# Weight preparation of a two-stage attention and gated-MLP kernel: earlier first loads, steps placed inside the stages, and another block order

## The chip, the cores and the metric

The kernel runs on one core of one Trainium2 chip. The metric is the device time of one execution in microseconds (us); less is better. The engines are named as the profile names them: PE is TensorE (matmuls; PEld its weight loads), DVE is VectorE, ACT is ScalarE, POOL is GpSimd, and SP is the engine from which every DMA of this kernel is issued. Each engine takes its instructions strictly in the order in which the kernel emits them.

## The reference

Two things are computed one after the other, all in 32-bit floating point, for 8 batch entries, 12 heads, 448 positions and head width 64:

```python
scores = scale * np.matmul(q, k.transpose(0, 1, 3, 2)) - np.log(S)
attn = 1.0 / (1.0 + np.exp(-scores))
x = np.matmul(attn, v)                       # heads side by side: 8 x 448 x 768

h = np.maximum(x @ w_in, 0.0)                # w_in: 768 x 1024
u, v = (h[..., :512], h[..., 512:])
v_n = (v - mu) / np.sqrt(var + 1e-06)        # mean and variance over the 512
v_s = np.einsum('ts,bsd->btd', w_spatial, v_n) + b_spatial[None, :, None]
out = (u * v_s) @ w_out                      # w_out: 512 x 768
```

## The kernel before, in words

**Precision.** Most products are made of three matmuls: each operand is split into a rounded high part and the low remainder (`split`, L98), and high times high, low times high and high times low are summed. So every weight has to be prepared on the chip before it can be used: it arrives as a raw 1024-word block in a work buffer, is converted by bit operations (`convert`, L107 to L133), and is written as a high and a low half into a constant tile. w_in and w_out arrive as 64-bit floating point, w_spatial as 32-bit.

**The stages.** The outer loop runs over four pairs of batch entries, m = 0 to 3. For each pair:

- *attention*: six iterations, each for two pairs of heads. In an iteration, scores for 7 key tiles are made on PE (psc; L226 for the short tile, L244 for the others), ACT takes the sigmoid (L252), and PE multiplies with v (pav, L282). The q/k blocks of the next iteration are cast and split (L100 and L101, tile qks), and the result is split into the constant tile x_s (L288 on ACT, L261 on DVE). The first two q/k blocks are used unsplit.
- *gate values* (`gate_values`): x times the second half of w_in, for seven tiles of 128 rows in four groups, (0,1), (2,3), (4,5) and (6). PE makes pv, ACT the relu rv (L315), DVE the statistics (L319, L320) and the subtraction of the mean (L325), POOL the reciprocal root (L322, L323), and DVE the normalised vn (L335, L336).
- *spatial* (`spatial`), for each of the two batch entries, in two pairs of output chunks: w_spatial times vn in PSUM (pg), then g = pg + bias on DVE (L372).
- *gated* (`gated`): x times the first half of w_in (pu), then g = relu(pu) * g on DVE (L394), then split into gs.
- *output* (`output`): gs times w_out (po) in three pairs of output chunks, copied by ACT (L422) and stored.

**Weights.** `weight_steps` is a Python generator over 22 steps: the six blocks of the gate half of w_in with four of w_spatial between them, six blocks of the other half of w_in, and six of w_out. It loads two steps ahead (`AHEAD`), through three work buffers (tag tmp for the first 13 steps, tag raw, shared with the q/k blocks, for the rest). Each `next` emits a part of a step up to the next `yield`. The first 13 steps (three parts for a block of w_in, one for a block of w_spatial, 31 in all) run on DVE alone: L113, L124, L127, then L129, L132, then L179, L180. The other nine have four parts: L113 and L120 on DVE; L122 on ACT; L129 and L132 on DVE; L176 on ACT. Their last subtraction (L180, DVE) is emitted together with the first part of the step behind.

In m = 0, `attention` asks for the 31 parts: two after the first scores, and then three at two places of every iteration, up to a budget. The main loop asks for four parts (`YB`) after each of the four gate groups, each spatial pair and each gated pair.

**What holds the order.** `in_program_order` binds every engine to the order of emission. PSUM is given out by rotation: three double buffers (ps2) for psc, pv, pg, pu and po, and two single ones (ps1) for pav. So the first pu of a pair takes the buffer of the fourth gate group, free when that group's rv has been read; the second pu takes that of the first spatial pair, free when its g has been added. DMAs all leave one queue, SP, in order; a DMA that waits for its work buffer holds those behind it.

**Block order of the weights.** A block of the first half of w_in holds all 512 output columns for 128 rows of the input; a pu product over all 768 rows for one chunk of 128 output columns therefore reads all six blocks. A block of w_out holds 512 consecutive values of the row-by-row flattened (4 x 768) columns.

Of the kernel before, what the change touches and what calls it, by code (L numbers as in the profile page):

```python
# [35 lines left out]
def attn_gmlp_kernel(  # L36
# [103 lines left out]
    def weight_steps():  # L140

        steps = []
        for i in range(NCC):
            steps += [(w_in, w_in_s, NCC + i)] + [(w_sp, w_sp_s, i)] * (i < NFC)
        steps += [(w_in, w_in_s, i) for i in range(NCC)]
        steps += [(w_out, w_out_s, i) for i in range(NFC * DM // 512)]
        raws = {}

        def load(n):
            if n < len(steps):  # L150
                src, _, i = steps[n]
                w = 512 if src is w_sp else 1024

                if n < NFIRST:
                    raw = work.tile([P, 1024], U32, tag="tmp", name=f"wraw_{n}", bufs=3)[:, :w]
                else:
                    raw = work.tile([P, 1024], U32, tag="raw", name=f"wraw_{n}", bufs=3)
                raws[n] = raw.bitcast(F32) if src is w_sp else raw
                nc.sync.dma_start(raws[n], src[:, i * w : (i + 1) * w])

        for n in range(AHEAD):
            load(n)
        for n, (src, dst, i) in enumerate(steps):
            load(n + AHEAD)
            if src is w_sp and i == 0:
                nc.sync.dma_start(b_bc, b_sp.broadcast_to([P, 512]))
            hi, lo = dst[:, i, 0], dst[:, i, 1]
            scalar = n >= NFIRST
            val = raws.pop(n)
            if src is not w_sp:  # L170
                raw = val
                val = work.tile([P, 512], U32, tag="wval", name=f"wval_{n}", bufs=2)
                yield from convert(val, raw, scalar)
                val = val.bitcast(F32)
            if scalar:
                nc.scalar.copy(hi, val)  # L176
                yield
            else:
                nc.vector.tensor_copy(hi, val)  # L179
            nc.vector.tensor_sub(lo, val, hi.bitcast(F32))  # L180
            if not scalar:
                yield
# [7 lines left out]
    def load_weights(n):  # L190
        for _ in range(n):
            next(weights, None)
# [98 lines left out]
    def product(ps, pairs, more=(), start=True, stop=True):  # L291

        ops = [(st(a), mv(c)) for st, mv in pairs for a, c in TERMS] + list(more)
        for i, (st, mv) in enumerate(ops):
            nc.tensor.matmul(ps, st, mv, start=start and i == 0, stop=stop and i == len(ops) - 1)  # L295

    vns = {}

    def gate_values(m, ts):

        n = len(ts)
        pv = banks(f"pv_{m}_{ts[0]}")
        for i, t in enumerate(ts):
            product(
                pv[:, i, :F],
                [
                    (
                        lambda a, cc=cc, t=t: x_s[:, a, cc, t * P : (t + 1) * P],
                        lambda c, cc=cc: w_in_s[:, NCC + cc, c, :],
                    )  # L310
                    for cc in range(NCC)
                ],
            )
        rv = work.tile([P, 2, 512], F32, tag="tmp", name=f"rv_{m}_{ts[0]}", bufs=3)
        nc.scalar.activation(rv[:, :n], pv[:, :n], AF.Relu)  # L315
        mv = work.tile([P, 2, 2], F32, tag="mv", name=f"mv_{m}_{ts[0]}")
        for i in range(n):
            stats = work.tile([P, 6], F32, tag="stats", name=f"stats_{m}_{ts[i]}")
            nc.vector.bn_stats(stats, rv[:, i])  # L319
            nc.vector.bn_aggr(mv[:, i], stats)  # L320
        rstd = work.tile([P, 2], F32, tag="rstd", name=f"rstd_{m}_{ts[0]}")
        nc.gpsimd.tensor_scalar_add(rstd[:, :n], mv[:, :n, 1], 1e-6)  # L322
        nc.gpsimd.tensor_tensor(rstd[:, :n], rstd[:, :n], mhalf[:, :n], op=ALU.pow)  # L323
        for i in range(n):
            nc.vector.tensor_scalar_sub(rv[:, i], rv[:, i], mv[:, i, 0:1])  # L325
        for i, t in enumerate(ts):
            vn = work.tile([P, 2, 512], F32R, tag="big", name=f"vn_{m}_{t}", bufs=7)
            if t != NFULL:
                parts = [(vn[:, 0], vn[:, 1], slice(0, P))]
            else:  # L330

                a, c = slice(0, HALF), slice(HALF, P)
                parts = [(vn[a, 0], vn[c, 0], a), (vn[c, 1], vn[a, 1], c)]
            for hi, lo, rows in parts:
                nc.vector.tensor_scalar_mul(hi, rv[rows, i], rstd[rows, i : i + 1])  # L335
                nc.vector.scalar_tensor_tensor(  # L336
                    lo,
                    rv[rows, i],
                    rstd[rows, i : i + 1],
                    hi.bitcast(F32),  # L340
                    op0=ALU.mult,
                    op1=ALU.subtract,
                )
            vns[t] = vn

    def cols_of(b):
        return slice(0, S) if b % 2 else slice(512 - S, 512)
# [3 lines left out]
    def spatial(b, fcs):  # L351

        odd = b % 2
        cols = cols_of(b)
        pg = banks(f"pg_{b}_{fcs[0]}")
        for i, fc in enumerate(fcs):
            fs = slice(fc * P, (fc + 1) * P)
            pairs = []
            for c in range(NFULL):
                vn = vns[c + 4 if odd else c]  # L360
                pairs.append(
                    (lambda a, vn=vn: vn[:, a, fs], lambda p, c=c: w_sp_s[:, c, p, cols])
                )

            short = vns[NFULL][:, odd, fs]
            product(
                pg[:, i, :S], pairs, [(short, w_sp_s[:, NFULL, a, cols]) for a in range(2)]
            )
        g = work.tile([P, 2, 512], F32, tag="tmp", name=f"g_{b}_{fcs[0]}", bufs=3)[:, :, :S]
        bb = b_bc[:, cols]  # L370
        bb = bass.AP(bb.tensor, bb.offset, [list(bb.ap[0]), [0, 2], list(bb.ap[1])])
        nc.vector.tensor_add(g, pg[:, :, :S], bb)  # L372
        gates[b, fcs] = g
# [3 lines left out]
    def gated(b, fcs, copy=nc.scalar.copy):  # L377

        odd = b % 2
        g = gates.pop((b, fcs))  # L380
        pu = banks(f"pu_{b}_{fcs[0]}")
        for i, fc in enumerate(fcs):
            fs = slice(fc * P, (fc + 1) * P)
            product(
                pu[:, i, :S],
                [
                    (
                        lambda a, cc=cc: w_in_s[:, cc, a, fs],
                        lambda c, cc=cc: x_s[:, c, cc, odd * S : (odd + 1) * S],
                    )  # L390
                    for cc in range(NCC)
                ],
            )
        nc.vector.scalar_tensor_tensor(g, pu[:, :, :S], 0.0, g, op0=ALU.max, op1=ALU.mult)  # L394
        gs = work.tile([P, 2, 2 * S], F32R, tag="split", name=f"gs_{b}_{fcs[0]}", bufs=3)
        gs = gs.rearrange("p a (i s) -> p a i s", i=2)
        split(gs[:, 0], gs[:, 1], g, copy)
        for i, fc in enumerate(fcs):
            hidden[b, fc] = gs[:, :, i]

    def output(b, es, parts=1):

# [2 lines left out]
        for part in range(parts):  # L405
            for i, e in enumerate(es):

                def weight(a, fc, e=e):
                    block, col = divmod(fc * DM + e * P, 512)
                    return w_out_s[:, block, a, col : col + P]  # L410

                product(
                    po[:, i, :S],
                    [
                        (lambda a, fc=fc: weight(a, fc), lambda c, fc=fc: hidden[b, fc][:, c])
                        for fc in range(part * n, (part + 1) * n)
                    ],
                    start=part == 0,
                    stop=part == parts - 1,
                )  # L420
# [17 lines left out]
    def attention(m):  # L438
# [20 lines left out]
        for n in range(first, end, 2):  # L459
# [20 lines left out]
            scores(n, odds)  # L480
            if direct:
                loads()
                weigh(2)
            ahead(attention_splits, n + 2, end)
            ahead(attention_splits, n + 3, end)
            vals(n, evens + short)
            weigh(3)
        vals(end - 2, odds)

    start_loads(0)  # L490
    pairs = [(0, 1), (2, 3)]
    running = attention(0)
    for m in range(B // 2):
        for _ in running:
            pass
        for ts in ((0, 1), (2, 3), (4, 5), (6,)):
            gate_values(m, ts)
            load_weights(YB)
        b0, b1 = 2 * m, 2 * m + 1
        more = m < B // 2 - 1  # L500
        for fcs in pairs:
            spatial(b0, fcs)
            load_weights(YB)
        for fcs in pairs:
            gated(b0, fcs)
            load_weights(YB)
        for fcs in pairs:
            spatial(b1, fcs)
            load_weights(YB)
        start_loads(m + 1)  # L510
        output(b0, (0, 1))
        output(b0, (2, 3))
# [64 lines left out]
```

## Time and profile before

| | us |
|---|---|
| runs before (three) | 708.11, 708.66, 708.86; median 708.66 |
| the profiled execution, its own time | 708.37 |
| its span, first to last instruction | 706.6 |
| PE busy | 686.4 |
| DVE busy | 283.1 |
| ACT busy | 250.3 |
| mean granted PE clock | 0.990 of full speed |

How to read the lines. In the chain of waits, a row is start, length, engine, tile, line and number of instructions. In the timeline, a row is start, length, engine, line, operation, output and inputs with their shapes, the number of instructions merged, and in brackets the idle time of the engine before it with what ended it. In a list of waits, the numbers are total time, times and longest. In a table of windows, a row is the window, its length, the busy time and number of instructions of the engine asked for, the granted PE clock as a share of full speed, the share of time in which the DMA engines were busy, and GB/s. PE's matmuls are pipelined, so their starts can lie 0.1 to 0.2 us apart from one view to another.

### The profile page before, as it was taken

To read this page: it belongs to the slowest core of one execution; us is meant where nothing else is said; L and a number is where in the kernel's file an instruction comes from. 1 tells how busy PE (TensorE), PEld (TensorE's weight loads), DVE (VectorE), ACT (ScalarE), POOL (GpSimd) and SP (SyncE) were. 2 spreads that over 40 slices of the span, in tenths; PEclk is the share of its full clock that TensorE was granted. 3 is DMA by queue.
4 is the path that set the end of the run, shared out by engine and by line. 5 is a ranking of instruction groups with operands and counts; after the bars stand their busy time and mean duration, and the time that the engine had idled before them with its cause. 6 is when DMAs were issued, how large, how long until landed. Compare 5 with 4: busy or idle time off the path is not lost.

```text
span 706.6 us, 8992 instructions
## 1 busy us (share of the span) xinstructions
PE 686.4 (97%) x3820; PEld 504.7 (71%) x3820; DVE 283.1 (40%) x448; ACT 250.3 (35%) x298; POOL 18.5 (3%) x36
## 2 busy tenths in 40 slices
PE   6899997989999999999999999999999999999997
PEld 2445686979855458899885447899986445889996
DVE  0899376761242416531313423633032441462120
ACT  6688211321366731011237771101125774101111
POOL 0000011000000001100000000100000000110000
PEclk9999998999999999999999999999999999999999
DMA  6675001241334210001234230000233230000102
GB/s 247 211 241 203 1 30 60 90 130 53 111 124 157 88 70 1 1 0 53 79 104 157 91 145 1 1 0 1 79 105 130 101 109 1 1 1 0 53 27 78
DMA packets 20248, 55.37 MB, mean 78 GB/s; under 512 B 1904, under 2 KB 8048, under 8 KB 20208
## 3 DMA queue, kind: packets, MB, share of 16 engines
q1 hardware_dynamic: 20208, 54.80, 22.3%
q8 instruction: 30, 0.49, 0.3%
q14 instruction: 10, 0.08, 0.0%
HBM read 43.78 MB, written 11.01 MB: 78 GB/s over the span
## 4 chain that ended last, share of the span: by engine, by line
PE 78%; DVE 3%; ACT 1%; issue 1%; ACTq 0%
PE po L295 16%; PE pav L282 15%; PE pu L295 14%; PE pv L295 12%; PE psc L244 10%; PE pg L295 8%; PE psc L226 2%; DVE wval L129 0%; DVE wval L132 0%; ACT wraw L122 0%; DVE gs L101 0%; DVE g L394 0%; DVE w_out_s L180 0%; DVE g L372 0%; ACT gs L100 0%
## 5 line engine op out<-in xcount | busy, mean ns | idle before, releaser
L252 ACT ACTIVATE at<-psc,bias_s 128x896 f32<-128x896 f32 x168 | 156.6, 1008 | 40.5 <-PE psc L226 25.3
L282 PE MATMUL pav<-at,v 128*64 128x448 f32 (+1 forms) x768 | 141.2, 553 | 0.0
L295 PE MATMUL po<-gs,w_out_s 128*128 128x448 f32 x576 | 122.2, 372 | 3.2 <-ACT w_out_s L176 2.6
L295 PE MATMUL pu<-x_s,w_in_s 128*128 128x448 f32 x576 | 120.4, 370 | 4.2 <-ACT rv L315 4.2
L295 PEld LDWEIGHTS po<-gs,w_out_s 128*128 128x128 f32 x576 | 109.1, 190 | 15.5 <-ACT w_out_s L176 2.9
L295 PEld LDWEIGHTS pu<-x_s,w_in_s 128*128 128x128 f32 x576 | 110.2, 191 | 13.4 <-ACT rv L315 4.5
L295 PE MATMUL pv<-w_in_s,x_s 128*128 128x512 f32 x504 | 115.4, 390 | 0.0
L295 PEld LDWEIGHTS pv<-w_in_s,x_s 128*128 128x128 f32 x504 | 94.3, 188 | 22.3 <-issue 2.8
L244 PEld LDWEIGHTS psc<-qks 64*128 64x128 f32 x828 | 73.1, 186 | 43.7 <-ACT at L252 16.8
L244 PE MATMUL psc<-qks 64*128 64x448 f32 x828 | 98.7, 379 | 4.4 <-DVE qks L101 4.4
L282 PEld LDWEIGHTS pav<-at,v 128*64 128x64 f32 (+1 forms) x768 | 42.2, 135 | 78.8 <-issue 73.9
L261 DVE TENSOR_TENSOR x_s<-pav,x_s 128x448 fp32r<-128x448 f32 x48 | 30.0, 624 | 126.8 <-ACT x_s L288 126.7
L295 PE MATMUL pg<-w_sp_s,vn 128*128 128x448 f32 x352 | 72.8, 365 | 0.0
L295 PEld LDWEIGHTS pg<-w_sp_s,vn 128*128 128x128 f32 x352 | 66.0, 187 | 5.8
L394 DVE SCALAR_TENSOR_TENSOR g<-pu,g 128x896 f32<-128x896 f32 x16 | 17.4, 1091 | 122.9 <-PE pu L295 122.9
L422 ACT COPY osb<-po 128x896 f32<-128x896 f32 x24 | 21.8, 909 | 121.5 <-PE po L295 110.9
L101 DVE TENSOR_TENSOR qks<-raw,qks 128x832 fp32r<-128x832 f32 x46 | 46.7, 1024 | 1.2
L100 ACT CAST gs<-g 128x896 fp32r<-128x896 f32 x12 | 11.3, 943 | 100.2 <-DVE g L394 100.2
L288 ACT CAST x_s<-pav 128x448 fp32r<-128x448 f32 x48 | 25.6, 534 | 55.4 <-PE pav L282 55.0
L315 ACT ACTIVATE rv<-pv 128x1024 f32<-128x1024 f32 (+1 forms) x16 | 14.7, 919 | 83.5 <-PE pv L295 83.5
L319 DVE BATCH_NORM_STATS2 stats<-rv 128x6 f32<-128x512 f32 x28 | 19.0, 679 | 49.3 <-ACT rv L315 49.3
L100 DVE CAST qks<-raw 128x832 fp32r<-128x832 f32 x36 | 21.1, 587 | 35.5 <-PE po L295 35.3
(36 smaller groups left out, 238.6 us busy)
## 6 DMA issues: line engine op xcount, KB each, us to landing
raw<-qk_dram SPq DMA_DIRECT2D x48, 448.0 KB, 3.6
v<-v_dram SPq DMA_DIRECT2D x24, 448.0 KB, 4.1
out_dram<-osb SPq DMA_DIRECT2D x24, 448.0 KB, 2.6
wraw<-w_in_dram SPq DMA_DIRECT2D x12, 512.0 KB, 4.0
wraw<-w_out_dram SPq DMA_DIRECT2D x6, 512.0 KB, 3.6
wraw<-w_sp_dram SPq DMA_DIRECT2D x4, 256.0 KB, 3.8
b_bc<-b_sp_dram SPq DMA_DIRECT2D x1, 256.0 KB, 3.6
```

What stands on the lines that cost most here:

```text
L100: copy(hi, src)
L101: nc.vector.tensor_sub(lo, src, hi.bitcast(F32))
L244: nc.tensor.matmul(psc[:, j, :S], st[rows, k : k + P], mv[rows, FULL:PART], start=i == 0, stop=i == len(ops) - 1,)
L252: nc.scalar.activation(at, psc[:, :, :S], AF.Sigmoid, bias=bias_s, scale=QK)
L261: nc.vector.tensor_sub(*late.pop(0))
L282: nc.tensor.matmul(pav[heads, :S], vt[rows, t, heads], at[rows, j], start=start, stop=stop)
L288: nc.scalar.copy(x[:, 0], pav)
L295: nc.tensor.matmul(ps, st, mv, start=start and i == 0, stop=stop and i == len(ops) - 1)
L315: nc.scalar.activation(rv[:, :n], pv[:, :n], AF.Relu)
L319: nc.vector.bn_stats(stats, rv[:, i])
L394: nc.vector.scalar_tensor_tensor(g, pu[:, :, :S], 0.0, g, op0=ALU.max, op1=ALU.mult)
L422: nc.scalar.copy(osb, po[:, :, :S])
```

## The change

The generator gets a `yield` right behind its first two loads, and the main program calls it once right behind the first q/k and v loads, so these two weight loads stand ahead of the fourth q/k load. In attention, the two parts after the first scores go. The calls of the main loop move into the stages: in a gate group, two parts ahead of the relu, one ahead of the vn operations, and one behind the first vn of the group; in a spatial pair, four parts ahead of g; in a gated pair, two ahead of g, one ahead of the split and one behind it. The number of parts per stage stays.

The host lays the first half of w_in and all of w_out out by pairs of output chunks: three blocks hold all that the first two chunks of u need, the next three what the last two need; and two blocks of w_out each hold all for one pair of output chunks. `half_of` finds chunk o's weights for row block k in the new order.

```diff
@@ weight_steps
         for n in range(AHEAD):
             load(n)
+        yield
         for n, (src, dst, i) in enumerate(steps):
             load(n + AHEAD)
@@
+    def half_of(w, o, k, n):
+
+        block, col = divmod((o // 2 * n + k) * 2 + o % 2, 4)
+        return w[:, block, :, col * P : (col + 1) * P]
+
@@ gate_values
                     for cc in range(NCC)
                 ],
             )
+        load_weights(2)
         rv = work.tile([P, 2, 512], F32, tag="tmp", name=f"rv_{m}_{ts[0]}", bufs=3)
...
             nc.vector.tensor_scalar_sub(rv[:, i], rv[:, i], mv[:, i, 0:1])
+        load_weights(1)
         for i, t in enumerate(ts):
...
             vns[t] = vn
+            if t % 2 == 0:
+                load_weights(1)
@@ spatial
                 pg[:, i, :S], pairs, [(short, w_sp_s[:, NFULL, a, cols]) for a in range(2)]
             )
+        load_weights(YB)
         g = work.tile([P, 2, 512], F32, tag="tmp", name=f"g_{b}_{fcs[0]}", bufs=3)[:, :, :S]
@@ gated
-                        lambda a, cc=cc: w_in_s[:, cc, a, fs],
+                        lambda a, cc=cc: half_of(w_in_s, fc, cc, NCC)[:, a],
...
+        load_weights(2)
         nc.vector.scalar_tensor_tensor(g, pu[:, :, :S], 0.0, g, op0=ALU.max, op1=ALU.mult)
+        load_weights(1)
         gs = work.tile([P, 2, 2 * S], F32R, tag="split", name=f"gs_{b}_{fcs[0]}", bufs=3)
         gs = gs.rearrange("p a (i s) -> p a i s", i=2)
         split(gs[:, 0], gs[:, 1], g, copy)
         for i, fc in enumerate(fcs):
             hidden[b, fc] = gs[:, :, i]
+        load_weights(1)
@@ output
-                def weight(a, fc, e=e):
-                    block, col = divmod(fc * DM + e * P, 512)
-                    return w_out_s[:, block, a, col : col + P]
...
-                        (lambda a, fc=fc: weight(a, fc), lambda c, fc=fc: hidden[b, fc][:, c])
+                        (
+                            lambda a, fc=fc: half_of(w_out_s, e, fc, NFC)[:, a],
+                            lambda c, fc=fc: hidden[b, fc][:, c],
+                        )
@@ attention
             if direct:
                 loads()
-                weigh(2)
...
-            weigh(3)
+            weigh(3 + (n + 2 == end))
         vals(end - 2, odds)
 
     start_loads(0)
+    load_weights(1)
@@ main loop
         for ts in ((0, 1), (2, 3), (4, 5), (6,)):
             gate_values(m, ts)
-            load_weights(YB)
...
             spatial(b0, fcs)
-            load_weights(YB)
...
             gated(b0, fcs)
-            load_weights(YB)
...
             spatial(b1, fcs)
-            load_weights(YB)
@@ host
-    w_in = np.transpose(moe_w_in.reshape(DM // P, P, 2, F), (1, 2, 0, 3)).reshape(P, -1)
-    w_out = np.transpose(moe_w_out.reshape(F // P, P, DM), (1, 0, 2)).reshape(P, -1)
+    w_in = np.transpose(moe_w_in.reshape(DM // P, P, 2, F), (1, 2, 0, 3))
+    w_u = np.transpose(w_in[:, 0].reshape(P, DM // P, F // 256, 256), (0, 2, 1, 3)).reshape(P, -1)
+    w_in = np.concatenate([w_u, w_in[:, 1].reshape(P, -1)], axis=1)
+    w_out = np.transpose(moe_w_out.reshape(F // P, P, DM // 256, 256), (1, 2, 0, 3)).reshape(P, -1)
```

## The prediction

> **What bounds the kernel now.** I read the shares and the slices first, then TensorE's waits, then the chain of waits, then the timeline around each wait.
>
> ```profile
> PE 686.4 (97%) x3820; PEld 504.7 (71%) x3820; DVE 283.1 (40%) x448; ACT 250.3 (35%) x298; POOL 18.5 (3%) x36
> ...
> PE   6899997989999999999999999999999999999997
> ```
>
> TensorE is the bound: busy for 686.4 of 706.6 us. The holes lie in the first quarter, and at the very end. The waits name the holes:
>
> ```profile
> PE psc L244 <- DVE qks L101: 4.4, 1, 4.4
> PE pu L295 <- ACT rv L315: 4.2, 1, 4.2
> PE psc L244 <- DMA raw<-qk_dram: 4.0, 1, 4.0
> PE po L295 <- ACT w_out_s L176: 2.6, 1, 2.6
> ```
>
> Apart from the first load (4.0), all belong to the weight preparation of the first batch pair. How much they cost in all, with the clock that they spoil, is read by holding the first pair against the second, which prepares nothing. The chain's rows (start, length) give the second pair, and the end of the first:
>
> ```profile
> 178.98 0.91 PE psc L226 x8
> ...
> 202.37 0.75 PE psc L226 x8
> ...
> 295.58 14.59 PE pu L295 x72
> ...
> 348.33 0.91 PE psc L226 x8
> ```
>
> From the second attention iteration of a pair (its L226) to the next pair's start is 348.33 - 202.37 = 145.96 us. In the first pair the same stretch runs from 14.80, in the next fence, to 178.98: 164.18 us. So **18.22 us** are there to be won, in three places. The timeline has place A, the windows its two iterations:
>
> ```profile
> 12.90 1.68 ACT L100 CAST qks<-raw 128x832 fp32r<-128x832 f32 x2
> ...
> 14.80 0.93 PE L226 MATMUL psc<-raw 64*64 64x448 f32 x8
> ...
> 16.70 0.43 DVE L113 TENSOR_SCALAR wval<-wraw 128x512 uint32<-128x512 uint32 x1 [15.82 <-DMA wraw<-w_in_dram]
> ...
> 19.43 1.95 DVE L101 TENSOR_TENSOR qks<-raw,qks 128x832 fp32r<-128x832 f32 x2
> ...
> 20.50 2.71 PE L244 MATMUL psc<-qks 64*128 64x448 f32 x16 [4.36 <-DVE qks L101]
> ```
> ```profile
> 14.80:31.53 16.73, 12.37 (x80) 0.90 0.67 231
> 31.53:42.12 10.59, 10.59 (x81) 1.00 0.78 253
> ...
> 146.37:149.87 3.50, 0.47 (x2) 1.00 0.08 12
> 149.87:154.87 5.00, 5.00 (x17) 0.66 0.67 228
> ```
>
> **A**: VectorE stands at L113 until the first weight load lands, and the q/k splits (L101) queue behind it. This iteration takes 16.73 us, the next, undisturbed, 10.59: 6.14 us, of them 4.36 idle and the rest slow clock. **B** lies between the first spatial products (pg) and the gated ones (pu):
>
> ```profile
> 87.57 0.85 DVE L325 TENSOR_SCALAR rv<-rv,mv 128x512 f32<-128x512 f32 x2
> 87.75 0.37 POOL L322 TENSOR_SCALAR rstd<-mv 128x2 f32<-128x2 f32 x1 [87.32 <-DVE mv L320]
> 88.19 0.79 POOL L323 TENSOR_TENSOR rstd<-rstd,mhalf 128x2 f32<-128x2 f32 x1
> 89.02 0.48 DVE L335 TENSOR_SCALAR vn<-rv,rstd 128x512 fp32r<-128x512 f32 x1 [0.60 <-POOL rstd L323]
> ...
> 102.89 0.69 DVE L180 TENSOR_TENSOR w_in_s<-wval,w_in_s 128x512 fp32r<-128x512 f32 x1
> ...
> 104.47 0.66 ACT L122 ACTIVATE wraw<-wraw 128x512 f32<-128x512 f32 x1 [8.45 <-issue]
> ...
> 105.16 0.69 DVE L129 SCALAR_TENSOR_TENSOR wval<-wraw,wval 128x512 uint32<-128x512 uint32 x1 [0.78 <-ACT wraw L122]
> 105.89 0.69 DVE L132 SCALAR_TENSOR_TENSOR wval<-wraw,wval 128x512 uint32<-128x512 uint32 x1
> ...
> 107.14 1.02 ACT L315 ACTIVATE rv<-pv 128x1024 f32<-128x1024 f32 x1
> ...
> 117.86 0.59 ACT L315 ACTIVATE rv<-pv 128x512 f32<-128x512 f32 x1
> ...
> 118.51 6.68 PE L295 MATMUL pu<-x_s,w_in_s 128*128 128x448 f32 x20 [4.17 <-ACT rv L315]
> 119.44 0.49 DVE L325 TENSOR_SCALAR rv<-rv,mv 128x512 f32<-128x512 f32 x1
> ...
> 120.09 0.58 POOL L323 TENSOR_TENSOR rstd<-rstd,mhalf 128x1 f32<-128x1 f32 x1
> ```
>
> The gated product pu takes the PSUM buffer of the fourth gate group, so it waits for that group's relu (rv, 117.86). That is late because VectorE and ScalarE run one weight step (L113 to L180, with two hand-overs) between any two groups. TensorE stops at 118.51 - 4.17 = 114.34, and pu's first 20 matmuls then take 0.33 us each, where 72 take 14.59 (0.20 each) in the second pair: the clock has dropped. C is the output product, waiting for the fourth and fifth block of w_out:
>
> ```profile
> 125.51 1.08 DVE L372 TENSOR_TENSOR g<-pg,b_bc 128x896 f32<-128x896 f32 x1
> ...
> 135.56 8.96 PE L295 MATMUL pg<-w_sp_s,vn 128*128 128x448 f32 x44
> ...
> 143.53 1.09 DVE L101 TENSOR_TENSOR gs<-g,gs 128x896 fp32r<-128x896 f32 x1 [1.01 <-ACT gs L100]
> ...
> 148.92 0.47 PE L295 MATMUL po<-gs,w_out_s 128*128 128x448 f32 x1 [2.55 <-ACT w_out_s L176]
> ```
>
> **B** from 114.34 to 135.56 is 21.22 us where the second pair's pu takes 14.59: 6.63 us. **C** is the remainder, 18.22 - 6.14 - 6.63 = 5.45 us, of which 3.03 idle (3.50 less 0.47 in the window row from 146.37).
>
> **The change, part by part.**
>
> Early loads. The first two weight loads (512 and 256 KB) leave the SP queue ahead of the fourth q/k load. That one waits for its buffer anyway; the DMA engines are idle just then:
>
> ```profile
> 5.00:6.00 1.00, 1.00 (x6) 1.00 0.98 380
> ...
> 9.00:10.00 1.00, 1.00 (x9) 1.00 0.00 0
> ```
>
> 786 KB at the 380 GB/s of the first row is 2.1 us, so they fill the hole. Cost 0; without that hole, at most these 2.1 us on the fourth q/k load.
>
> Steps in attention. The two steps ahead of the first splits go, the rest keep their count (31, by the budget) and end at the same place, in the last iteration. L101 can then follow the q/k casts on ScalarE at about 13.8 and be done with the first split at 14.8, before TensorE's first use of it (20.50 - 4.36 = 16.14): gain 6.14. What could be late next is VectorE itself: its windows of two undisturbed iterations show
>
> ```profile
> 31.11:42.12 11.01, 10.56 (x20) 1.00 0.77 250
> ...
> 52.70:63.29 10.59, 10.25 (x19) 1.00 0.69 251
> ```
>
> so up to 10.56 of 11.01 and 10.25 of 10.59 us. It kept pace there, with the same groups of three steps between the splits; I carry the same margin over, and take 0, with 6.14 as the other end.
>
> The layout. The first pu pair needs only the three blocks that attention has prepared, the second pair the other three, where each needed all six; an output pair needs two of six w_out blocks, where it needed four. The two of the first output product are prepared when g ends (123.6, below), 16 us before that product: C goes. The instructions are the same in number and size: cost 0.
>
> Steps inside the gate groups. Half of a step (subtraction, L113, L120, ScalarE's L122) now stands ahead of rv, so rv is queued on ScalarE behind L122, and the PSUM buffer behind rv. L129 and L132 stand where VectorE waits for GpSimd, and the cast to w_in_s leaves the path. Per group: the stretch from L122's end (104.47 + 0.66 = 105.13) to rv (107.14), 2.01 us, is taken out; L129 and L132 put 0.73 + 0.69 us in a gap of 0.60; less 0.15, by which VectorE's neighbours overlap (two L325 of 0.49 take 0.85), 0.66 net. Gain 1.35, for the three groups ahead of the fourth rv 4.05, less the 0.6 us subtraction that joins the first: 3.45. So rv moves from 117.86 to 114.41 (times here without A's shift), and pu can start 0.65 later, as now, at 115.06: **0.73 us** of the 4.17 stay.
>
> Step inside the spatial stage. The bias addition g (L372), which frees the buffer for the second pu pair, keeps a whole step ahead of it, as now. rv to g's end is 125.51 + 1.08 - 117.86 = 8.73, plus 0.49 for L129 and L132 in the last group's wait (1.42 less 0.15 overlap, less the 0.78 from L325's end at 119.93 to vn behind L323, 120.09 + 0.58 + 0.04): g ends at 114.41 + 9.22 = 123.63. The first pu pair, warm, ends at 115.06 + 7.30 = 122.36, so TensorE waits again, **1.33 us** with the hand-over. This stall is new; now pu is so late that g is never missed. Behind it the output product wants the last hidden split. From g's end to that split VectorE takes 143.53 + 1.09 - 126.59 = 18.0 us now, of which two waits of 0.78 (L122) and two of 1.01 (the cast of gs) are filled by the new order: 14.4, so 138.0, against 123.69 + 7.30 + 8.96 = 139.95 for the product. Cost 0, by a margin of 1.9.
>
> The one cost without a row: GpSimd's L322 and L323 now run beside L129 and L132. If neither hinders the other, L323 (ends 88.98) is done before VectorE is ready for vn (88.36 + 0.72 + 0.61 = 89.69): 0. If L323 has to wait for both, it ends at 88.36 + 0.72 + 0.69 + 0.58 = 90.35: 0.70 us per group. The nearest rows are L322's: in the pair it ends at 88.12, just behind the first L325 (87.57 + 0.47); so it seems to have waited out one instruction and then slipped in. By that L323 would end near 89.63, free of cost if L132 goes on beside it, 0.56 late if not. I take 0.3 per group, four groups: **1.2 us**.
>
> Sum, against the profiled execution's own 708.37: 708.37 - 18.22 + 0.73 + 1.33 + 1.2 = 693.4. The runs' median lies 0.29 higher: **693.7 us**. Later pairs get the same instructions as now.
>
> The stalls that stay are 1.6 and 1.6 us with the 0.3 in them; I add no slow clock, since the shortest idle time that slowed it here was 3.03 in 3.50 us (window row 146.37). The Trainium skill, page "TensorE: Matmul & The Clock Gate", section "HAM oscillation — how this bites in real kernels", puts the limit at gaps of about 3.4 us; place C shows it somewhat lower.
>
> **The rivals.**
>
> 1. GpSimd is shut out, or shuts VectorE out: 0.70 in each of four groups, 2.8 in place of 1.2, so 695.3; the first stall is then 2.8 us, and if it slows the clock, the second pair's wait hides most of that: up to 696. For it: L322's ends. Against it: L323 with VectorE beside it took only 0.21 more than alone, and on two columns for one. The Trainium skill, page "SBUF — State Buffer", section "Who interferes with whom", has it as a rule: a VectorE instruction with two SBUF inputs, such as L129 and L132, and a GpSimd instruction that reads SBUF exclude each other. By that rule this rival's time holds; no run here shows such a pair side by side.
>
> 2. VectorE binds attention: it has 0.3 to 0.5 us of slack per iteration, and the 6.14 us saved are taken from its time too. The worst is that attention ends where it does now: 693.7 + 6.14 = 699.8. Against it: two of the 31 steps go from its start to its end, and the first splits start 5.6 us earlier.
>
> 3. The rearrangement of the groups does nothing: the order on VectorE and ScalarE is merely shifted, rv stays at 117.86 relative to attention. B stays 6.63 in place of 3.26: 697.1.
>
> 4. Slower: the clock. If short stalls in a row kept TensorE at half clock from pu to the end of the output product, 14.59 + 8.96 + about 14.8 = 38 us of work would take 38 us more: 732. It decides from 15 us lost, 30 us at half clock. Against it: each drop here was over within 5 to 6 us of dense work, at 149.87 to 154.87 within the window.
>
> **How the numbers follow.** Forecast (cost per group between 0 and 0.45): 0.53, its own range 692.2 to 694.6. Rival 1: 0.26. Rival 2: 0.08. Rival 3: 0.07. Rival 4: 0.02. The remaining 0.04 is for something unseen of either sign. The range 691.6 to 699.0 takes in the forecast, rivals 1 and 3, and half of rival 2. A measurement of this kernel tells about 0.2% (1.4 us) from no change: faster 0.95, same 0.02, slower 0.03.
>
> **What would show it.** Right: no TensorE wait on qks; the second iteration at 10.6 us; everything behind it 6.1 us earlier; two waits of 1 to 2 us, at pu on rv and then on L372's g; no wait on w_out_s; the clock full from 10 us on. L323's end against L132's tells the forecast from rival 1. Wrong: a wait on qks in a later iteration, a first pu wait above 3 us, slow clock behind it, or po waiting for a hidden split.

## The result, and the profile after

| | before | after |
|---|---|---|
| median of the runs, us | 708.76 | 692.66 |
| lowest to highest, us | 708.11 to 709.72 | 692.46 to 693.21 |
| the profiled execution, us | 708.37 | 692.46 |
| its span, us | 706.6 | 690.7 |
| PE busy, us | 686.4 | 680.6 |

The changed kernel takes 0.9773 of the time before (95% interval 0.9756 to 0.979), 16.1 us less. The forecast was 693.7.

The shares and slices of the changed kernel's profile:

```profile
PE 680.6 (99%) x3820; PEld 500.6 (72%) x3820; DVE 282.1 (41%) x448; ACT 250.2 (36%) x298; POOL 18.8 (3%) x36
...
PE   7999999999999999999999999999999999999997
```

TensorE runs the same 3820 matmuls in 5.8 us less busy time, mainly because the slow clock behind the three waits is gone, and its idle time went from 20.2 to 10.1 us. Line numbers have moved by up to 13 with the edit: relu rv is L322, the mean's subtraction L332, GpSimd's two instructions L329 and L330, vn L343 and L344, g L383. TensorE's waits in the changed kernel:

```profile
PE psc L245 <- DMA raw<-qk_dram: 4.0, 1, 4.0
PE pu L296 <- DVE g L383: 1.0, 1, 1.0
PE pu L296 <- ACT rv L322: 0.4, 1, 0.4
```

The first load's wait stays. Those on qks and on w_out_s are gone (the two blocks of w_out that the first output product needs are ready at 117.90, and it starts at 133.56); the one on rv fell from 4.2 to 0.4; one on g is new. Two stretches of its timeline carry this, first the start:

```profile
13.05 1.68 ACT L100 CAST qks<-raw 128x832 fp32r<-128x832 f32 x2
13.98 1.96 DVE L101 TENSOR_TENSOR qks<-raw,qks 128x832 fp32r<-128x832 f32 x2 [13.10 <-ACT qks L100]
14.96 0.93 PE L227 MATMUL psc<-raw 64*64 64x448 f32 x8
...
15.82 2.15 PE L245 MATMUL psc<-qks 64*128 64x448 f32 x18
...
16.39 0.42 DVE L113 TENSOR_SCALAR wval<-wraw 128x512 uint32<-128x512 uint32 x1
...
25.54 0.93 PE L227 MATMUL psc<-raw 64*64 64x448 f32 x8
```

The splits now follow the casts, VectorE's first weight step comes behind them without a wait, and the iteration takes 25.54 - 14.96 = 10.58 us. Then the gate groups:

```profile
81.59 0.85 DVE L332 TENSOR_SCALAR rv<-rv,mv 128x512 f32<-128x512 f32 x2
81.76 0.36 POOL L329 TENSOR_SCALAR rstd<-mv 128x2 f32<-128x2 f32 x1 [81.33 <-DVE mv L327]
82.21 0.80 POOL L330 TENSOR_TENSOR rstd<-rstd,mhalf 128x2 f32<-128x2 f32 x1
82.35 0.69 DVE L129 SCALAR_TENSOR_TENSOR wval<-wraw,wval 128x512 uint32<-128x512 uint32 x1
83.08 0.69 DVE L132 SCALAR_TENSOR_TENSOR wval<-wraw,wval 128x512 uint32<-128x512 uint32 x1
83.69 0.48 DVE L343 TENSOR_SCALAR vn<-rv,rstd 128x512 fp32r<-128x512 f32 x1
...
108.14 0.58 ACT L322 ACTIVATE rv<-pv 128x512 f32<-128x512 f32 x1
...
108.77 7.56 PE L296 MATMUL pu<-x_s,w_in_s 128*128 128x448 f32 x36 [0.42 <-ACT rv L322]
...
110.10 0.68 DVE L129 SCALAR_TENSOR_TENSOR wval<-wraw,wval 128x512 uint32<-128x512 uint32 x1
110.35 0.87 POOL L330 TENSOR_TENSOR rstd<-rstd,mhalf 128x1 f32<-128x1 f32 x1
110.82 0.69 DVE L132 SCALAR_TENSOR_TENSOR wval<-wraw,wval 128x512 uint32<-128x512 uint32 x1
111.43 0.48 DVE L343 TENSOR_SCALAR vn<-rv,rstd 128x512 fp32r<-128x512 f32 x1
...
116.22 1.08 DVE L383 TENSOR_TENSOR g<-pg,b_bc 128x896 f32<-128x896 f32 x1
...
117.36 7.56 PE L296 MATMUL pu<-x_s,w_in_s 128*128 128x448 f32 x36 [1.03 <-DVE g L383]
```

In the pair, GpSimd's power (L330) ends at 83.01, while L129 still runs; in the single group it ends at 111.22, during L132. Both times vn comes straight behind L132. TensorE's two waits stand where the forecast had put them.

### The profile page after: what moved, and what is told of

It is laid out like the page before. It is cut to its first block, busy times and chain, and to the rows that moved or that the text cites. A ratio compares the mean times of both kernels' runs of the same rounds, so it can differ in the third digit from the quotient of the medians.

```text
span 690.7 us, 8989 instructions
## 1 busy us (share of the span) xinstructions
PE 680.6 (99%) x3820; PEld 500.6 (72%) x3820; DVE 282.1 (41%) x448; ACT 250.2 (36%) x298; POOL 18.8 (3%) x36
## 4 chain that ended last, share of the span: by engine, by line
PE 93%; DVE 5%; ACT 1%; DMA 0%; issue 0%; ACTq 0%
PE pav L283 20%; PE po L296 17%; PE pu L296 16%; PE psc L245 15%; PE pv L296 14%; PE pg L296 9%; PE psc L227 3%; DVE vn L344 1%; DVE stats L326 1%; ACT rv L322 1%; DVE wval L132 1%; DVE vn L343 0%; DMA raw<-qk_dram 0%; DVE wval L129 0%; DVE rv L332 0%
## 5 line engine op out<-in xcount | busy, mean ns | idle before, releaser
L296 PE MATMUL po<-gs,w_out_s 128*128 128x448 f32 x576 | 120.1, 368 | 0.2
L296 PE MATMUL pu<-x_s,w_in_s 128*128 128x448 f32 x576 | 118.3, 365 | 1.4 <-DVE g L383 1.0
L296 PEld LDWEIGHTS pu<-x_s,w_in_s 128*128 128x128 f32 x576 | 108.0, 188 | 10.7 <-DVE g L383 1.4
L322 ACT ACTIVATE rv<-pv 128x1024 f32<-128x1024 f32 (+1 forms) x16 | 14.7, 917 | 81.3 <-PE pv L296 81.3
```

## The experiments

Two theories stood at the start. Theory 1: each of the three waits has one cause, and one part of the change takes it away (start: both edits together; gate groups: the new places; w_out: the layout). Theory 2: a wait can have several cures in this change, so that parts of it are not needed. Beside them the disputed price, GpSimd beside VectorE, and what the two waits that stay consist of.

### The start of attention

**no_early_loads**

```diff
         for n in range(AHEAD):
             load(n)
-        yield
...
     start_loads(0)
-    load_weights(1)
```

> The changed kernel without its early weight loads: they leave the SP queue where they did before, behind the loads of the first attention iteration; the two steps ahead of the first splits stay away. Theory 1 (the splits only have to stand ahead of the steps): VectorE reaches its first step at 16.4 anyway, and these loads landed at 16.7 in the kernel before, so 692.7 to 693.0 us, no TensorE wait on qks. Theory 2 (the loads have to come early): the 4.4 us wait on qks is back, near 698.8.

**keep_two_steps**

```diff
             if direct:
                 loads()
+                weigh(2)
```

> The changed kernel with the two steps back ahead of the first splits, the early loads kept. Theory 1 (the loads in time are enough): the first load lands near 9.5, VectorE is through its two steps (2.8 us) near 12.3, before the q/k cast that the splits wait for ends at 13.9: 692.7 us. Theory 2 (steps ahead of the splits delay them whatever the loads do): a wait on qks, up to 6.1 us more, 698.8.

**no_start**: both of these edits.

> The changed kernel with neither early loads nor the steps moved: only the start of attention is as before. Both theories: the wait of 4.4 us on qks and the slow clock behind it are back, 692.7 + 6.1 = 698.8 us, the second iteration 16.7 us. If VectorE had been the bound of attention, less than 6.1 would come back.

What these texts call two steps are two parts of the first step, as `weigh(2)` asks for them.

Measured: 692.68 (0.9771 of the time before, 0.9754 to 0.9787), 692.63 (0.9768, 0.9753 to 0.9782) and 699.56 us (0.9863, 0.9845 to 0.988). The lists of the first two have no wait on qks. That of the last one shows the old wait back in its place, beside those of the changed kernel:

```profile
PE psc L244 <- DVE qks L101: 4.0, 1, 4.0
PE psc L244 <- DMA raw<-qk_dram: 4.0, 1, 4.0
PE pu L295 <- DVE g L382: 1.0, 1, 1.0
PE pu L295 <- ACT rv L321: 0.4, 1, 0.4
```

Either part of the change takes the wait away; together they do no more than one. Their timelines say why. Without the early loads, VectorE waits 0.66 us for the first weight, but behind the splits:

```profile
13.50 1.96 DVE L101 TENSOR_TENSOR qks<-raw,qks 128x832 fp32r<-128x832 f32 x2 [12.62 <-ACT qks L100]
...
16.65 0.43 DVE L113 TENSOR_SCALAR wval<-wraw 128x512 uint32<-128x512 uint32 x1 [0.66 <-DMA wraw<-w_in_dram]
```

With the two steps kept and the loads early, the steps fit in ahead of the cast:

```profile
10.09 0.43 DVE L113 TENSOR_SCALAR wval<-wraw 128x512 uint32<-128x512 uint32 x1 [9.21 <-DMA wraw<-w_in_dram]
...
12.22 0.69 DVE L132 SCALAR_TENSOR_TENSOR wval<-wraw,wval 128x512 uint32<-128x512 uint32 x1
...
14.50 1.96 DVE L101 TENSOR_TENSOR qks<-raw,qks 128x832 fp32r<-128x832 f32 x2 [1.59 <-ACT qks L100]
```

Place A came back in no_start: 6.9 us by the medians, each of which is good to about 1.2 us, where 6.1 was expected. The prediction's stretch, from the second attention iteration to the first pair's end, is 153.98 us in its profiled execution and 148.13 in the changed kernel's, 5.85 more, with a wait of 4.04 us in place of 4.36. So VectorE was not the bound of attention.

### The layout and the order

**no_layout**: the changed kernel with the block order of before, on the host and in `gated` and `output`.

```diff
-                        lambda a, cc=cc: half_of(w_in_s, fc, cc, NCC)[:, a],
+                        lambda a, cc=cc: w_in_s[:, cc, a, fs],
...
-                            lambda a, fc=fc: half_of(w_out_s, e, fc, NFC)[:, a],
...
+                        (lambda a, fc=fc: weight(a, fc), lambda c, fc=fc: hidden[b, fc][:, c])
...
```

> The changed kernel with the block order of before; the order of the steps stays changed. Theory L (the prediction: the layout takes the wait for w_out_s away): the first output product needs the fifth block again and waits, up to the 5.5 us of place C, 698.2. Theory O (the order alone does it): in the trace of the changed kernel the fifth block is ready at 131.95, the output product starts at 133.56, and the gated product starts after all of w_in is ready: 692.7, no wait on w_out_s.

**layout_only**: the reverse of this on the kernel before.

> The kernel before with the new block order alone. If the layout by itself removes place C: the two blocks of the first output product are ready at 126.5 and 131.8, 708.8 - 5.4 = 703.3 us, the waits on qks and rv stay. If it needs the new order too: 708.8.

**order_only**: no_layout with the edits of no_start as well, so that of the change only the new places of the steps inside the stages are left.

> The kernel before with the steps placed inside the stages alone (old start, old block order). Theory O (the order cures both B and C): 708.8 - 6.6 - 5.4 + 1.45 of waits that stay = 698.2 us, only the wait on qks as before. Theory L (C needs the layout): 698.2 to 703.6, with a wait on w_out_s.

Measured: no_layout 693.21 us (0.977, 0.9754 to 0.9786), as fast as the changed kernel. layout_only 704.26 us (0.9931, 0.9913 to 0.995). order_only 699.59 us (0.9862, 0.9843 to 0.988). Neither of the last two waits for w_out_s. In order_only the wait on rv has fallen to 0.4 us, in layout_only it is the old one: place B is cured by the new places of the steps, not by the layout. The waits of layout_only:

```profile
PE psc L244 <- DVE qks L101: 4.3, 1, 4.3
PE pu L295 <- ACT rv L320: 4.2, 1, 4.2
PE psc L244 <- DMA raw<-qk_dram: 4.0, 1, 4.0
```

and the timeline of no_layout, where the fifth block's subtraction (L181) ends 1.6 us ahead of the output product that may read it:

```profile
131.91 0.68 DVE L181 TENSOR_TENSOR w_out_s<-wval,w_out_s 128x512 fp32r<-128x512 f32 x1
...
134.17 6.12 PE L296 MATMUL po<-gs,w_out_s 128*128 128x448 f32 x29
```

So place C had two cures too. By itself the layout is worth 4.5 us of the 5.4 expected (the interval holds 5.4; the profiled stretch is 5.0 shorter); once the steps stand inside the stages it is worth nothing that can be measured: the stretch is 148.13 us in no_layout as in the changed kernel. order_only and no_start measure the same, which says it again: they differ by the layout alone.

### GpSimd beside VectorE

**pool_beside**

```diff
+        load_weights(1)
         for i in range(n):
             nc.vector.tensor_scalar_sub(rv[:, i], rv[:, i], mv[:, i, 0:1])
-        load_weights(1)
```

> The changed kernel with L129 and L132 of a gate group ahead of the subtraction of the mean, so that GpSimd's first instruction starts together with L129 in every group, its second beside L132. If the two engines do not hinder each other: GpSimd's add and power take about 0.1 and 0.6 us, vn starts when VectorE is ready, 692.7 us. If they exclude each other: each of GpSimd's two ends behind a VectorE instruction, and vn or the instructions beside them come up to 0.7 us per group later, up to 695.3.

**pool_alone**

```diff
             nc.vector.tensor_scalar_sub(rv[:, i], rv[:, i], mv[:, i, 0:1])
-        load_weights(1)
...
             if t % 2 == 0:
-                load_weights(1)
+                load_weights(2)
```

> The changed kernel with L129 and L132 behind the first vn of a group, not where VectorE waits for GpSimd. If filling that wait is worth what the prediction counted: VectorE idles 0.6 us again in each of four groups, the waits at pu grow from 1.45 to about 3.9 us, 695.1 us. If GpSimd's power was slowed by them as much as they saved: 692.7.

pool_beside was run once: 693.01 us. GpSimd is slowed, and a good deal; VectorE's instructions are not. GpSimd's rows of its timeline, VectorE's, and TensorE's waits:

```profile
81.49 0.57 POOL L329 TENSOR_SCALAR rstd<-mv 128x2 f32<-128x2 f32 x1 [81.06 <-DVE mv L327]
82.14 1.39 POOL L330 TENSOR_TENSOR rstd<-rstd,mhalf 128x2 f32<-128x2 f32 x1
```
```profile
81.31 0.66 DVE L129 SCALAR_TENSOR_TENSOR wval<-wraw,wval 128x512 uint32<-128x512 uint32 x1
82.01 0.69 DVE L132 SCALAR_TENSOR_TENSOR wval<-wraw,wval 128x512 uint32<-128x512 uint32 x1
82.61 0.88 DVE L333 TENSOR_SCALAR rv<-rv,mv 128x512 f32<-128x512 f32 x2
83.56 0.49 DVE L343 TENSOR_SCALAR vn<-rv,rstd 128x512 fp32r<-128x512 f32 x1
```
```profile
PE pu L296 <- DVE g L383: 1.1, 1, 1.1
PE pu L296 <- ACT rv L322: 0.9, 1, 0.9
```

The add ends at 82.06, 0.09 us behind L129; the power, which takes 0.80 us on its two columns in the changed kernel, takes 1.39 and ends 0.04 us behind the last L333 (the mean's subtraction, here one line further down). So here GpSimd waits out VectorE's instructions, those with two inputs in SBUF (L129) among them, and the power waits out three in a row. VectorE's own instructions stay within 0.03 us of their usual length.

Something is lost by it all the same. vn needs the power and starts 0.03 us behind its end. From the start of the first instruction behind the statistics to vn are 83.56 - 81.31 = 2.25 us, where the changed kernel takes 83.69 - 81.59 = 2.10. Over the three groups ahead of the fourth rv this adds up: from the first rv to the fourth are 29.71 us in place of 29.23, and the wait on rv is 0.90 us in place of 0.42. So the truth lies between the two readings, 0.16 us per group where full exclusion was put at up to 0.7; the time of one run can't show half a microsecond.

pool_alone: 696.8 us (0.9827, 0.981 to 0.9845), 4.1 us above the changed kernel where 2.4 was expected. Its waits and its windows by microseconds (window, length, busy, clock, DMA share, GB/s):

```profile
PE pu L296 <- ACT rv L322: 2.5, 1, 2.5
PE pu L296 <- DVE g L382: 1.4, 1, 1.4
```
```profile
110.00:111.00 1.00, 0.27 (x1) 0.59 0.01 4
111.00:112.00 1.00, 1.00 (x3) 0.50 0.00 0
112.00:113.00 1.00, 1.00 (x4) 0.50 0.00 0
113.00:114.00 1.00, 1.00 (x5) 0.70 0.00 0
114.00:115.00 1.00, 1.00 (x7) 1.00 0.00 0
```

The waits are as expected, 3.9 us in place of 1.45. The expectation left out the clock: a wait of 2.48 us was enough to halve it for some 3 us, and the first pu pair took 8.88 us where it takes 7.56 in the changed kernel. 2.4 of wait and 1.3 of slow clock are 3.7 us, which is what the profiled stretch is longer by (151.84 for 148.13). So filling GpSimd's gap is worth what was counted, and the clock on top.

### The two waits that stay

**g_ahead**

```diff
-        load_weights(YB)
+        load_weights(2)
         g = work.tile([P, 2, 512], F32, tag="tmp", name=f"g_{b}_{fcs[0]}", bufs=3)[:, :, :S]
...
         gates[b, fcs] = g
+        load_weights(2)
```

> The changed kernel with the bias addition g of a spatial pair between the halves of a step instead of behind the whole step: VectorE does it while ScalarE has L122. g ends near 115.2 instead of 117.3, before the first gated pair ends at 116.3. If the second wait is g's place alone: it goes, 1.03 us, 691.6 us; the first wait of 0.4 us stays.

**rv_ahead**

```diff
-        load_weights(2)
+        load_weights(1)
         rv = work.tile([P, 2, 512], F32, tag="tmp", name=f"rv_{m}_{ts[0]}", bufs=3)
         nc.scalar.activation(rv[:, :n], pv[:, :n], AF.Relu)
+        load_weights(1)
```

> The changed kernel with ScalarE's relu rv ahead of L122 instead of behind it. rv no longer waits for VectorE; VectorE's statistics start when rv and L120 are both done. If the chain through L122 sets the first wait: rv comes about 0.6 us earlier per group, the wait on rv goes (0.4 us) and g's wait shrinks by 1 us or more, 691.2 us. If L122 behind rv delays L129 as much: 692.7.

**both_ahead**: both edits.

> Both of these edits. If the two waits are all that the weight preparation still costs TensorE: no wait but the first load's, 692.7 - 1.45 = 691.2 us, the clock full throughout. If something else is late next: above 691.5 with a new wait named.

Measured: g_ahead 691.51 us (0.9761, 0.9746 to 0.9776), its only wait beside the first load the 0.4 us on rv. rv_ahead 690.82 us (0.975, 0.9736 to 0.9765; lowest to highest 690.46 to 690.96). both_ahead 690.69 us (0.9749, 0.9733 to 0.9764). The waits of rv_ahead:

```profile
PE psc L245 <- DMA raw<-qk_dram: 3.9, 1, 3.9
```

rv_ahead alone takes both waits away: g waited for VectorE's whole chain, and that hung on rv standing behind L122. So the wait on g has two cures as well, and g_ahead adds nothing to rv_ahead. rv_ahead is the version to keep: its runs lie all below the changed kernel's, though the two ratios' intervals still overlap. The medians are 1.8 us apart, of which up to 0.6 may lie outside the kernels, since the kernel before ran at 708.20 beside these runs and at 708.76 beside the changed kernel's. The profiled stretch leaves the start of the execution out and shows more: 148.13 us in the changed kernel, 146.84 in g_ahead, 146.15 in rv_ahead and 146.16 in both_ahead, against 348.33 - 202.19 = 146.14 in the second pair of the kernel before, which prepares nothing. (202.19 is that iteration's start in the timeline; the chain of waits has it at 202.37.) By this rv_ahead is worth 2.0 us and leaves nothing to win in this stretch. Among kernels that should not differ in it (no_early_loads, keep_two_steps, no_layout and the changed kernel) it goes from 148.13 to 148.57, so it is good to some 0.4 us.

## Why the prediction was right

**The 18.22 us to be won, in three places.** Right but for a detail: the first pair's start was read from the timeline (14.80) and the second pair's from the chain (202.37), which in the second pair lie 0.18 us apart, so 18.04 would be like for like. The offset drops out of a comparison of the two kernels. In the same two views the stretch is now 163.09 - 14.96 = 148.13 us (this chain row ends the first pair in the changed kernel), so 2.17 us of the 18.22 are left (1.99 of the 18.04):

```profile
163.09 0.91 PE psc L227 x8
```

**Steps in attention, 6.14 us.** Right in size: 16.73 to 10.58. VectorE kept pace, with 10.25 us of work in an iteration of 10.59 (windows of the changed kernel):

```profile
46.70:57.29 10.59, 10.25 (x19) 1.00 0.71 237
```

The reason was half the story: the text counted the moved steps as the gain and the early loads as free, where either would have done. The diff's `weigh(3 + (n + 2 == end))` plays no part in it: at that place one part is left of the budget of 31, whichever number is asked for.

**The layout, C goes.** C went, all of it. The layout alone would take it away (layout_only), but as the cause in this kernel it was wrong: no_layout has no wait either. The prediction had itself worked out that VectorE would be through its steps earlier, but never asked when the fifth block would be ready in the old layout.

**The gate groups, 0.73 us of 4.17 left.** The mechanism and the size hold (4.17 - 3.45 is 0.72): from the start of pg to that of pu are 108.77 - 99.11 = 9.66 us where the same 44 matmuls of pg take 9.08 in the second pair's chain, so 0.58 (0.42 of it in the wait's own row).

```profile
99.11 9.24 PE L296 MATMUL pg<-w_sp_s,vn 128*128 128x448 f32 x44
```

**The new wait on g, 1.33 us.** It is there: 117.36 - 108.77 - 7.30 = 1.29 us.

**GpSimd, 1.2 us.** This term was mis-sized: it is 0 in the changed kernel, the lower end of the 0 to 0.45 per group that the forecast allowed. GpSimd is through before VectorE comes to vn: the power ends at 83.01 and at 111.22, vn starts at 83.69 and at 111.43. In the pair the power takes 0.80 us beside L129, as long as in the kernel before (0.79), where VectorE stood idle behind the last L325. The reading of L322's rows (waits out one instruction, then slips in) fits the add in pool_beside, but not the power there, which waited out L132 and both L333. When GpSimd gets in beside VectorE stays open. Rival 1 needed exclusion both ways, or GpSimd shut out until L132's end; neither came in the changed kernel. The Trainium skill's rule, page "SBUF — State Buffer", section "Who interferes with whom", by which the two exclude each other, holds for GpSimd in pool_beside (0.57 us in place of the 0.36 beside one L332, 1.39 in place of 0.80), but not for the power beside L129 in the changed kernel. Its other half, that VectorE blocks when GpSimd was first, is not seen in that pair either, where L129 started 0.14 us behind the power and took its usual 0.69.

**The clock.** Full from 10 us on, as forecast. But the step "the shortest idle time that slowed it here was 3.03" gave no safe side: in pool_alone 2.48 us did. The page "TensorE: Matmul & The Clock Gate", section "HAM oscillation — how this bites in real kernels", of the Trainium skill puts the limit near 3.4 us; the 2.48 measured here is well below, and it decides. Rival 4 did not occur: the clock stayed at 1.00 behind the two short waits, and even in pool_alone it came back within some 3 us of dense work.

**The sum.** 708.37 - 18.22 + 2.17, and 0.16 us by which attention's second iteration began later (14.96 for 14.80), is 692.5, the profiled execution's 692.46. The forecast's 693.4 on that basis is 0.9 too high: 1.2 for GpSimd and 0.2 in the two waits too much, 0.3 of the stretch (0.18 of it the offset of the two views) and the 0.16 at the start too little. Part of the error cancels by chance: the total is off by less than the GpSimd term alone.

## What to carry to other kernels

Before a wait is put down to one cause, ask for every part of the edit whether it alone would take the wait away: here two of the three waits had two cures, and the layout or the early loads could be left out (each was tried, both together were not). Fill a wait of one engine with work that the path needs anyway, but keep what frees a buffer for the bound engine (rv here) ahead of the filler on its own queue, which was worth another 2 us. A short stall on TensorE is priced with its clock: here waits of 1.03 and 1.35 us cost their own length, 2.48 us cost half as much again.

## What the runs showed of the hardware that was not expected

- A wait of 2.48 us between dense matmuls halved TensorE's granted clock for about 3 us (pool_alone); 1.35 us in the same run, and 1.03 in the changed kernel, did not. Where between them the limit lies, and whether it is the same in every run, stays open.
- GpSimd's power on a 128x2 operand took 0.80 us beside the end of L332 and nearly all of L129 (changed kernel), no longer than without L129 (0.79, kernel before), but 1.39 us beside L132 and two L333, ending 0.04 us behind them (pool_beside). On 128x1 it took 0.58 us beside an idle VectorE, 0.87 beside L129 and L132 (changed kernel) and 1.00 beside L132 and one L333 (pool_beside). VectorE's instructions beside it kept their length to 0.03 us.
- The second iteration of attention starts between 14.40 us (no_early_loads) and 15.77 (both_ahead) in these profiles. The first twelve matmuls, of the same shapes, take 3.99 us in the one and 4.85 in the other, 0.33 and 0.40 us each, where twelve of the same kind a little later take 2.53 (0.21 each) in both. The granted clock stands at 1.00 in these windows all the while, so the profile doesn't show the slow start as a lowered clock. Where the full speed sets in differs from run to run by as much as the last edits are worth, so a single profile's whole span doesn't rank them.
